# One square moved from VectorE to ScalarE at the end of the attention of batch 0

## The chip, the cores and the metric

One core of one Trainium2 chip. The metric is the device time of one execution in microseconds (us). Profiles were taken with each kernel. Positions inside a kernel are us from the start of the profiled span.

## The reference

```python
# q, k, v: (8 batches, 12 heads, 448 positions, 64)
scores = np.matmul(q, k.transpose(0, 1, 3, 2)) / np.sqrt(64)
attn   = np.maximum(scores, 0.0) ** 2 / 448        # ReLU, then a square; no softmax
x      = np.matmul(attn, v)                        # -> (3584 tokens, 768)
h      = x @ w_in                                  # 768 -> 2048
g      = np.maximum(h, 0) + alpha * np.minimum(h, 0)
out    = g @ w_out                                 # 2048 -> 768
```

## The kernel before

Heads are taken in quads (four heads of one batch; three quads make a batch), and a quad's scores in seven chunks `j`. A chunk runs through three engines: TensorE makes the scores, ScalarE or VectorE takes the ReLU into a bf16 tile `rl`, and the square goes into `at`, from which TensorE makes the product with V. Squares are done in pairs, two chunks in one VectorE instruction. Batch 0 has 21 chunks, so the last, chunk 6 of quad 2, is left without a partner, and is squared alone:

```python
def squares(keep=0, single=None):

    while len(todo) >= 2 + keep or todo and single is not None:
        m = min(len(todo), 2)
        some = [todo.pop(0) for _ in range(m)]
        t = some[0][2]
        a = at_pool.tile([128, 2, 2, S], BF16, tag="at", name="at")
        if m == 2:
            nc.vector.tensor_tensor(a, t, t, ALU.mult)                       # line 196
        else:
            cur.clear()
            if single is nc.scalar:
                nc.scalar.activation(a[:, 0], t[:, 0], ACTF.Square)          # line 200
            else:
                nc.vector.tensor_tensor(a[:, 0], t[:, 0], t[:, 0], ALU.mult) # line 202
        ...
def attnv(n, js=range(NJ), space=sc_ps, apart=False):
    ...
    for j in js:
        a = att.pop((n, j))
        for r in range(2):
            for s in range(2):
                nc.tensor.matmul(half[r][64 * s:64 * s + 64, :S],            # line 223
                                 vb[n][64 * r:64 * r + 64, s, j, :],
                                 a[64 * r:64 * r + 64, s],
                                 start=(j == 0), stop=(j == NJ - 1))
    ...  # then the rescale into xT, half on ScalarE (line 232), half on VectorE (line 234)
```

The end of batch 0's attention, with the first matmuls of the MLP put among it:

```python
# last quad, last chunks:
            if last and j > 4:
                ffn1(0, j - 5, range(0, 4))
            if last and j == 6:
                ffn1(0, 2, range(0, 4))
...
    squares(single=nc.vector)              # the line that changes
    attnv(2, range(0, 4), apart=True)
    attnv(2, range(4, NJ))
    ffn1(0, 3, range(0, 4))
...
    for ff in range(4):
        ffn1(0, ff, range(4, KM))          # these need the rescaled product
```

## Time and profile before

| | before |
|---|---|
| median, range of 3 runs | 390.79 us, 390.65 to 391.74 us |
| profiled span | 389.6 us |
| TensorE busy | 97% |
| VectorE / ScalarE busy | 65% / 55% |
| granted clock of TensorE | 1.0 |

What matters is not these shares but one place, 22 to 29 us, in the view of instructions in order of time; the prediction below shows it. A line there has the start, the duration, the engine, the source line, the operation, its output and inputs, the number of merged instructions, and, in brackets, how long the engine was idle before and what ended that.

One more number is the time from the start of the last two groups of MLP matmuls ahead of the product (eight matmuls of line 255; 23.23 us in the kernel before) to the first matmul of the MLP's second layer (line 271). From the view in order of time, 44 to 56 us, of the kernel before:

```profile
45.41 1.46 PE L271 MATMUL ops<-w_out_sb,gT 128*128 128x384 bf16 x8
```

The **stretch** is 45.41 - 23.23 = 22.18 us.

### The profile page before, as it was taken

What the parts mean: (1) busy time and instruction counts of PE and PEld (TensorE: products, weight loads), DVE (VectorE), ACT (ScalarE), POOL (GpSimd) and SP (SyncE); (2) the same over time, 40 slices, a digit from 0 to 9 for tenths busy, and PEclk for the clock granted to TensorE, in tenths of its full rate; (3) what the DMA queues carried; (4) which work ended last, traced back from release to release, by engine and by line L of the source; (5) the groups of instructions that cost most, each with busy time, mean ns of one, the idle gap of its engine ahead of it and who ended that gap; (6) DMA issues with size and microseconds to landing.
All of it is one profiled execution on the core that took longest, in us unless ns stands there. A gap on an engine that the chain in (4) does not pass through costs nothing.

```text
span 389.6 us, 7873 instructions
## 1 busy us (share of the span) xinstructions
PE 379.5 (97%) x3210; PEld 214.8 (55%) x3210; DVE 253.2 (65%) x336; ACT 215.5 (55%) x361; POOL 74.9 (19%) x89
## 2 busy tenths in 40 slices
PE   6799999999999999999999999999999999999996
PEld 4345556545655456645665456654566545655564
DVE  4986877687687757766675666777676376726411
ACT  5965767464566656664473645756565366624200
POOL 7654000052251114201221012301030000000000
PEclk9999999999999999999999999999999999999999
DMA  8999997894995519825494354937253220130033
GB/s 163 191 209 204 204 216 264 235 300 100 259 258 182 126 65 240 222 65 164 94 260 150 67 164 98 278 126 174 29 91 87 70 47 2 42 81 2 0 82 81
DMA packets 64755, 55.43 MB, mean 142 GB/s; under 512 B 35776, under 2 KB 60496, under 8 KB 64720
## 3 DMA queue, kind: packets, MB, share of 16 engines
q1 hardware_dynamic: 53504, 44.78, 44.7%
q0 software_dynamic: 10976, 9.96, 16.1%
q8 instruction: 25, 0.41, 0.4%
q10 hardware_dynamic: 240, 0.20, 0.2%
q14 instruction: 10, 0.08, 0.1%
HBM read 45.62 MB, written 11.01 MB: 145 GB/s over the span
## 4 chain that ended last, share of the span: by engine, by line
PE 93%; ACT 2%; DMA 2%; DVE 1%; POOL 1%; issue 0%; POOLq 0%; DVEq 0%
PE hps L255 37%; PE ops L271 37%; PE avh L223 7%; PE sc L156 6%; PE sch L156 3%; DMA qe<-in_q_dram 2%; PE ops L294 1%; PE av L223 1%; PE tps L131 1%; ACT rl L185 1%; DVE at L196 1%; ACT xT L232 0%; POOL ke L357 0%; POOL ke L355 0%; POOL qe L355 0%
## 5 line engine op out<-in xcount | busy, mean ns | idle before, releaser
L255 PE MATMUL hps<-xT,w_in_sb 128*128 128x448 bf16 x768 | 149.2, 353 | 0.6 <-ACT xT L232 0.4
L271 PE MATMUL ops<-w_out_sb,gT 128*128 128x384 bf16 x864 | 145.8, 326 | 0.0
L263 DVE SCALAR_TENSOR_TENSOR gT<-neg,beta_sb,hps 128x448 bf16<-128x448 f32 x128 | 85.7, 679 | 58.3 <-ACT neg L262 57.5
L271 PEld LDWEIGHTS <-gT 128*128 128x128 bf16 x864 | 83.4, 98 | 61.2 <-issue 7.9
L255 PEld LDWEIGHTS <-w_in_sb 128*128 128x128 bf16 x768 | 74.0, 98 | 72.5 <-issue 5.5
L262 ACT ACTIVATE neg<-hps 128x448 f32<-128x448 f32 x128 | 69.1, 546 | 63.7 <-PE hps L255 63.6
L185 ACT ACTIVATE rl<-sc 128x896 bf16<-128x896 f32 x87 | 77.1, 923 | 44.1 <-PE sc L156 44.0
L196 DVE TENSOR_TENSOR at<-rl 128x1792 bf16<-128x1792 bf16 x80 | 85.7, 1113 | 2.1 <-ACT rl L185 0.9
L106 DVE COPY osb<-ops 128x384 f32<-128x384 f32 x30 | 16.7, 557 | 45.6 <-PE ops L271 45.6
L163 ACT ACTIVATE rl<-sch 128x448 bf16<-128x448 f32 x81 | 41.6, 550 | 4.7 <-PE sch L156 4.6
L106 POOL CAST kb<-kraw 128x896 bf16<-128x896 f32 x16 | 18.8, 1178 | 114.5 <-DMA kT<-kb 55.9
L156 PE MATMUL sc<-qT,kT 64*64 64x448 bf16 x456 | 36.1, 355 | 3.1 <-ACT rl L185 1.4
L223 PE MATMUL avh<-at,vb 64*64 64x448 bf16 x588 | 34.4, 350 | 0.4 <-DVE at L196 0.4
L156 PEld LDWEIGHTS <-kT 64*64 64x64 bf16 x672 | 21.8, 106 | 19.6 <-issue 13.2
L104 ACT COPY osb<-ops 128x384 f32<-128x384 f32 x24 | 11.4, 476 | 36.0 <-PE ops L271 36.0
L223 PEld LDWEIGHTS <-vb 64*64 64x64 bf16 x672 | 25.7, 106 | 9.8 <-issue 5.2
L183 DVE TENSOR_SCALAR rl<-sc 128x896 bf16<-128x896 f32 x27 | 29.4, 1089 | 0.6 <-PE sc L156 0.6
L106 POOL CAST vb<-vraw 128x896 bf16<-128x896 f32 x16 | 15.9, 991 | 36.8 <-PE avh L223 36.7
L106 POOL CAST qb<-qraw 128x896 bf16<-128x896 f32 x16 | 16.6, 1040 | 32.3 <-DMA qT<-qb 28.0
L156 PE MATMUL sch<-qT,kT 64*64 64x448 bf16 x216 | 22.5, 355 | 0.0
L165 DVE TENSOR_SCALAR rl<-sch 128x448 bf16<-128x448 f32 x27 | 16.8, 622 | 2.8 <-PE sch L156 0.8
L238 DVE TENSOR_SCALAR xT<-avh 128x448 bf16<-128x448 f32 x19 | 11.9, 624 | 7.7 <-PE avh L223 7.7
(59 smaller groups left out, 98.4 us busy)
## 6 DMA issues: line engine op xcount, KB each, us to landing
out_dram<-osb SPq DMA_DIRECT2D x54, 192.0 KB, 2.8
qraw<-in_q_dram SPq DMA_DIRECT2D x19, 448.0 KB, 5.3
kraw<-in_k_dram SPq DMA_DIRECT2D x18, 448.0 KB, 4.4
vraw<-in_v_dram SPq DMA_DIRECT2D x18, 448.0 KB, 6.1
w_out_sb<-in_moe_w_out_dram POOLq DMA_DIRECT2D x2, 1536.0 KB, 20.0
w_in_sb<-in_moe_w_in_dram POOLq DMA_DIRECT2D x8, 192.0 KB, 8.7
w_in_sb<-in_moe_w_in_dram POOLq DMA_DIRECT2D x4, 384.0 KB, 9.8
vb<-in_v_dram POOLq DMA_DIRECT2D x6, 224.0 KB, 9.6
```

The lines of the kernel that those rows point to most:

```text
L106: eng.tensor_copy(o, i)
L156: nc.tensor.matmul(half[r][64 * c:64 * c + 64, :S], kT[n][64 * r:64 * r + 64, j, c, :], qT[n][64 * r:64 * r + 64, :, c, :], start=True, st ...
L163: nc.scalar.activation(rl[:, r], half[r][:, :S], ACTF.Relu)
L165: nc.vector.tensor_scalar(rl[:, r], half[r][:, :S], 0.0, None, ALU.max)
L183: nc.vector.tensor_scalar(rl, ps[:, :, :S], 0.0, None, ALU.max)
L185: nc.scalar.activation(rl, ps[:, :, :S], ACTF.Relu)
L196: nc.vector.tensor_tensor(a, t, t, ALU.mult)
L223: nc.tensor.matmul(half[r][64 * s:64 * s + 64, :S], vb[n][64 * r:64 * r + 64, s, j, :], a[64 * r:64 * r + 64, s], start=(j == 0), stop=(j ...
L255: nc.tensor.matmul(ps, w_in_sb[:, km // 2, km % 2, bass.ts(ff, 128)], xT[b][:, km // 2, km % 2, :], start=(km == 0), stop=(km == KM - 1))
L262: nc.scalar.activation(neg, ps, ACTF.Relu, scale=-1.0)
L263: nc.vector.scalar_tensor_tensor(gT[b // 2][:, ff, (b % 2) * S:(b % 2) * S + S], neg, beta_sb[:, ff:ff + 1], ps, ALU.mult, ALU.add)
L271: nc.tensor.matmul(ps, gT[sb][:, ff, bass.ts(c, 128)], w_out_sb[:, ff, bass.ts(hf, 384)], start=(ff == 0), stop=(ff == KF - 1))
```

## The change

The intent: at that place VectorE still has two pair squares to do before it comes to the single one, while ScalarE is done with its ReLUs and idle. ScalarE is to take it, so that the chunk is ready sooner.

```diff
-    squares(single=nc.vector)
+    squares(single=nc.scalar)
     attnv(2, range(0, 4), apart=True)
     attnv(2, range(4, NJ))
     ffn1(0, 3, range(0, 4))
```

## The prediction

> **What bounds the kernel now.** I read three things in order: the page's busy shares, the chain that ended last, and then the instructions in time order around the moved one.
>
> The busy shares:
>
> ```profile
> PE 379.5 (97%) x3210; PEld 214.8 (55%) x3210; DVE 253.2 (65%) x336; ACT 215.5 (55%) x361; POOL 74.9 (19%) x89
> ...
> PE 93%; ACT 2%; DMA 2%; DVE 1%; POOL 1%; issue 0%; POOLq 0%; DVEq 0%
> ```
>
> TensorE is busy 379.5 us of 389.6 us, and 93% of the chain that ended last is TensorE work. All idle time of TensorE together is 389.6 - 379.5 = 10.1 us, so a change that only moves vector work can win at most a part of these 10.1 us: the part that lies where it acts. Most of it lies in the first 22 us: the stretch 0 to 16 us has 11.41 us of TensorE work (4.6 us idle) and 16 to 22 us has 4.54 us (1.5 us idle). The stretch 24 to 28 us, where the moved instruction lies, has 4.00 us of TensorE work in 4.00 us.
>
> Now the instructions in order of time there. The two ReLU lines are from a window that shows the second of a merged pair apart; the rest is the opening 32 us:
>
> ```profile
> 23.35 0.92 ACT L185 ACTIVATE rl<-sc 128x896 bf16<-128x896 f32 x1
> 24.03 1.08 DVE L196 TENSOR_TENSOR at<-rl 128x1792 bf16<-128x1792 bf16 x1
> ...
> 23.23 1.69 PE L255 MATMUL hps<-xT,w_in_sb 128*128 128x448 bf16 x8
> 24.85 1.52 PE L223 MATMUL av<-at,vb 64*64 64x448 bf16 x28
> 25.04 0.62 DVE L202 TENSOR_TENSOR at<-rl 128x896 bf16<-128x896 bf16 x1
> 25.05 1.16 POOL L407 DMA_DIRECT2D w_out_sb<-in_moe_w_out_dram  x1 [0.28 <-DMA w_in_sb<-in_moe_w_in_dram]
> 26.30 2.44 PE L255 MATMUL hps<-xT,w_in_sb 128*128 128x448 bf16 x12
> 26.40 0.54 ACT L232 ACTIVATE xT<-av 128x448 bf16<-128x448 f32 x1 [2.13 <-PE av L223]
> 26.45 0.62 DVE L234 TENSOR_SCALAR xT<-av 128x448 bf16<-128x448 f32 x1 [0.79 <-PE av L223]
> ```
>
> What to see: the square of the last chunk (line 202, the only row of it here) starts on VectorE at 25.04, straight behind the two pair squares that VectorE still had to do, and ends at 25.66. ScalarE has made the chunk's ReLU by 23.35 + 0.92 = 24.27 and then stands idle for 2.13 us, until 26.40. So the operand is ready 0.77 us before VectorE comes to it, on an engine that has nothing else to do. That is plainly why one would move it.
>
> But TensorE has no gap there: 23.23 to 24.92, 24.85 to 26.37, 26.30 to 28.74 follow on each other without a wait. When does it need the chunk? The last quad's attention-times-V product is 28 matmuls, seven chunks of four, and the chunk in question is the seventh. The view by tile has the first of the 28 at 24.8 and the last at 26.0; evenly spread, 24.85 + 6 x (1.52 - 0.35)/6 = 26.02 us for the last group of four (0.35 us is one matmul's duration, the four of a group run side by side). Against 25.66 the square is ready **some 0.36 us before it is needed**. The list of what TensorE waited for between 22 and 60 us says the same; it is complete, and the square is not in it:
>
> ```profile
> PE hps L255 <- ACT xT L232: 0.4, 1, 0.4
> PE hps L255 <- DVE gT L263: 0.2, 1, 0.2
> ```
>
> The first of these is the wait at 22.05 for an earlier quad's rescaled output; the second is the wait at 28.96 for a PSUM buffer that the first activation of the MLP frees. Both have other producers than the moved square.
>
> **What the Trainium skill says.** "ScalarE: Activation LUTs", section "What ACT_TABLE_LOAD costs": an activation with immediate scale and bias takes 186 ns + 0.833 ns per element, so 932 ns for 896 elements; and every switch to another table set costs about 2.66 us. The trace agrees on the first: the six squares that ScalarE already does later in this kernel take 950 ns. On the second, the trace has a single table load, at 0.73 us, and those six squares run later without another, mixed with ReLUs and copies. So the new one needs no switch either:
>
> ```profile
> L200 ACT ACTIVATE at<-rl x6: 950/950/951, 112.9 to 339.4; 128x896 bf16<-128x896 bf16 x6
> L362 ACT ACT_TABLE_LOAD x1 | 1.3, 1283 | 0.7 <-PEq L555 0.7
> ```
>
> "VectorE: DVE Perf Modes", section "Side-by-side: where the cycles go for N=2048 bf16": two elements per cycle plus about 158 cycles for fill and decode, so (448 + 158)/0.96 = 631 ns for 896 bf16 elements; the trace has 618 to 626 ns for the two of them. So the operation becomes longer by about 0.33 us where it moves, and only its earlier start can make up for that.
>
> "SBUF — State Buffer", section "Who interferes with whom": VectorE with two SBUF inputs contends with GpSimd instructions that read SBUF. The moved square lay beside GpSimd's issue of the first half of the output weights (25.05, 1158 ns). The trace does not show a cost: the issue of the second half at 33.0, with no such square beside it, took 1158 ns too.
>
> "Perfetto Trace Analysis", section "Optimization Strategy": find the gaps of the engine that one optimizes for and what blocks it there. That is what the list above does; it finds no gap at this place.
>
> **The change part by part.** Built and compared instruction by instruction, the changed kernel has one row fewer on VectorE (line 202, 128x896), one more on ScalarE (line 200, between its last ReLU of the quad and the rescale of line 232), and the same TensorE, GpSimd and SyncE rows. The one altered wait is that of the first matmul of the last chunk: on ScalarE where it was on VectorE.
>
> - Removed from VectorE: 1 x 0.62 us, at 25.04 to 25.66. What VectorE does next is line 234, which waits for the end of the matmuls at 26.37 and starts at 26.45. So VectorE's idle time before it grows from 0.79 to about 1.3 us (26.45 less the 25.11 at which its last pair square ends), and line 234 starts as before. Worth 0.
> - Added to ScalarE: 1 x 0.95 us, from about 24.30 (the ReLU's end and a small semaphore delay) to 25.25. ScalarE's next is line 232 at 26.40, so its idle time there shrinks from 2.13 to about 1.1 us and line 232 starts as before. Cost 0.
> - The chunk is ready at about 25.25 instead of 25.66: 0.4 us earlier. The matmul that needs it starts at 26.02, because TensorE is then busy with the six chunks before. Slack 0.77 instead of 0.36 us. Gain 0.
> - Nothing behind it moves: the four matmuls end at 26.37 and the two rescales wait for that.
>
> The sum is 0 + 0 + 0 = **0.0 us**. The time stays at its 390.79 us; three runs of the same kernel lay between 390.65 and 391.74, so the range has to be that of the noise.
>
> **The rivals.**
>
> Rival 1, the chunk was on the path after all. TensorE's ends are modelled in the profile and the wait of the moved matmul could be hidden in the stated 1.52 us. For it: that the ends are modelled. Against: groups of 28 like it later in the chain take 1.47 us, this one 1.45 us, so it holds no hidden wait. If it were so, 0.1 to 0.4 us would be won: 390.4 to 390.7 us, 0.1%.
>
> Rival 2, ScalarE's square comes late or holds up the rescale of line 232, on which the next matmuls depend. For it: it is 0.33 us longer, and ScalarE is in order, so anything late in it delays line 232. Against: its operand is ready at 24.27, and it would have to end after 26.0 to hold up the matmul, after 26.4 to hold up the rescale; it would need to start 0.8 us late. If it did: up to +0.3 us.
>
> Rival 3, the timing of loads. The opening third is heavy with transfers (DMA engines busy nine tenths), and the first half of the output weights, issued at 25.05, takes 18.3 us, so lands at 43.4, 2.0 us before the first matmul that reads any of it at 45.4. If the missing VectorE instruction lets GpSimd write its descriptors sooner, that load could land a little earlier, but nothing waits for it now; the order of transfers does not change. Expected 0; through jitter of the opening loads (one DMA wait, 5.85 us from 4.32, is on the chain) several tenths of a us either way, in both kernels alike.
>
> Even if every one of these were added up, they stay under 1 us, or 0.25%; 2% is 7.8 us, over twelve times the whole instruction that was removed.
>
> **Range and chances.** Centre 390.8 us, the median before with a step of zero. The low end 390.1 allows rival 1 in full and a fast draw; the high end 391.8 allows a draw like the slowest of the three before, or rival 2. Within 2%: 0.98; faster and slower 0.01 each, for what I do not foresee.
>
> **What would show it right or wrong.** Right: in the profile after, line 200 on ScalarE at about 24.3 for 0.95 us; ScalarE's idle before line 232 down from 2.1 to about 1.1 us, VectorE's before line 234 up from 0.8 to about 1.3 us or a little more; the 28 matmuls still from 24.85 to 26.37 relative to the matmuls before them, with no TensorE wait for ScalarE's square; one table load; TensorE idle about 10 us in all. Wrong: a TensorE wait named after line 200 or longer than 0.1 us between 24 and 29 us; a second table load (about +1.3 to 2.7 us); matmuls of the last chunk that start clearly earlier than before, which would mean that the square had been on the path. A change of the total by over 1 us with this stretch unchanged would have to be noise or the opening loads.

## The result

| | before | after |
|---|---|---|
| median (6 runs each) | 390.92 us | 390.94 us |
| range | 390.5 to 391.74 us | 390.67 to 393.12 us |
| ratio, 95% interval | | 1.0008, 0.9986 to 1.0029 |

Ratios are the mean time of one kernel's runs over that of the other's of the same rounds, so not quite the ratio of the medians quoted. The time lies in the predicted range.

The profiled run of after happened to be the 393.12 us one, with a span of 391.3 us against 389.6. Its page, then instructions of it in order of time:

```profile
PE 381.7 (98%) x3210; PEld 215.7 (55%) x3210; DVE 251.7 (64%) x335; ACT 216.3 (55%) x362; POOL 74.9 (19%) x89
...
PEclk9699999999999999999999999999999999999999
```

```profile
24.91 1.69 PE L255 MATMUL hps<-xT,w_in_sb 128*128 128x448 bf16 x8
24.92 1.16 POOL L407 DMA_DIRECT2D w_out_sb<-in_moe_w_out_dram  x1 [0.26 <-DMA w_in_sb<-in_moe_w_in_dram]
25.98 0.95 ACT L200 ACTIVATE at<-rl 128x896 bf16<-128x896 bf16 x1
26.53 1.52 PE L223 MATMUL av<-at,vb 64*64 64x448 bf16 x28
28.09 0.54 ACT L232 ACTIVATE xT<-av 128x448 bf16<-128x448 f32 x1 [1.15 <-PE av L223]
28.13 0.62 DVE L234 TENSOR_SCALAR xT<-av 128x448 bf16<-128x448 f32 x1 [1.63 <-PE av L223]
...
47.09 1.46 PE L271 MATMUL ops<-w_out_sb,gT 128*128 128x384 bf16 x8
```

Read the last two views against those of before. The square is on ScalarE now (line 200, 0.95 us) and ends 0.40 us after the product's first matmul starts (25.98 + 0.95 - 26.53), where on VectorE it ended 0.81 us after (25.66 - 24.85). So the chunk **is** ready 0.41 us sooner. Yet the 28 matmuls take their 1.52 us as before, and the stretch is 47.09 - 24.91 = 22.18 us, to the hundredth what it was. What TensorE waits for from 22 to 60 us is the same two lines, 0.4 and 0.2 us, that the prediction shows for the kernel before.

All of the 1.7 us by which this span is longer lies ahead of the square: the MLP matmuls of the stretch start at 24.91 here and at 23.23 before (1.68 us). The row of granted clock goes with it: the second slice (about 10 to 20 us) reads 6, not 9. In slices of one microsecond the clock of after is 0.50 from 11 to 17 us, while that of before is 1.00 there. (This run also waits 1.5 us for a load at about 9 us; but behind it TensorE is only 0.22 us later than in before, at 10.43 against 10.21, so 1.46 us of the 1.68 come after it.) None of this can come from an instruction that starts at 26 us; the first experiment and a run of the kernel before itself (393.06 us, at the same mean clock of 0.989) confirm it.

### The profile page after: what moved, and what is told of

Same layout as the page of the kernel before. It is cut to its first block, busy times and chain, and to the rows that moved or that the text cites. A ratio compares the mean times of both kernels' runs of the same rounds, so it can differ in the third digit from the quotient of the medians.

```text
span 391.3 us, 7873 instructions
## 1 busy us (share of the span) xinstructions
PE 381.7 (98%) x3210; PEld 215.7 (55%) x3210; DVE 251.7 (64%) x335; ACT 216.3 (55%) x362; POOL 74.9 (19%) x89
## 4 chain that ended last, share of the span: by engine, by line
PE 95%; DMA 2%; ACT 1%; POOL 1%; issue 0%; DVE 0%; POOLq 0%
PE hps L255 37%; PE ops L271 37%; PE avh L223 8%; PE sc L156 6%; PE sch L156 3%; DMA qe<-in_q_dram 2%; PE ops L294 1%; PE tps L131 1%; PE av L223 1%; ACT rl L185 1%; ACT rl L163 0%; POOL ke L357 0%; POOL ke L355 0%; POOL qe L355 0%; DVE gT L263 0%
## 5 line engine op out<-in xcount | busy, mean ns | idle before, releaser
L196 DVE TENSOR_TENSOR at<-rl 128x1792 bf16<-128x1792 bf16 x80 | 84.8, 1103 | 2.1 <-ACT rl L185 0.9
L106 POOL CAST kb<-kraw 128x896 bf16<-128x896 f32 x16 | 19.7, 1230 | 117.0 <-DMA kT<-kb 53.9
L223 PE MATMUL avh<-at,vb 64*64 64x448 bf16 x588 | 35.5, 360 | 0.0
L106 POOL CAST vb<-vraw 128x896 bf16<-128x896 f32 x16 | 16.7, 1044 | 37.3 <-PE avh L223 37.1
L106 POOL CAST qb<-qraw 128x896 bf16<-128x896 f32 x16 | 15.0, 934 | 31.4 <-DMA qT<-qb 31.4
```

The costliest lines, as they stand in the source:

```text
L106: eng.tensor_copy(o, i)
L223: nc.tensor.matmul(half[r][64 * s:64 * s + 64, :S], vb[n][64 * r:64 * r + 64, s, j, :], a[64 * r:64 * r + 64, s], start=(j == 0), stop=(j ...
```

## The experiments

Ten kernels were run, 5 rounds each beside the kernel before on the same chip (4 to 6 runs of each). One execution of each was profiled, so a stretch is a single reading; those that should be alike differ by 0.01 us. Three views were read from each: the waits of TensorE, the instructions in order of time, and the stretch defined above. The theory, **S**: the square has slack on both engines, so its move buys nothing. The rivals: **C**, it is on the path and the profile hides it; **B** and **A**, as told with each run.

### The changed kernel once more

No edit.

> The changed kernel once more, for a profile whose opening ran at full granted clock (the first one had 0.84 there). Theory S (slack): the moved square was ready before TensorE needed it on either engine, so the time is that of before, ratio 1.000 within 0.002; counted from the first matmul of the last quad's attention-times-V product, the square ends at +0.40 us on ScalarE (it ended at +0.81 on VectorE) and the last four matmuls still begin at +1.17. Rival C (critical after all): faster by 0.1 to 0.4 us. Rival N (the 1.7 us longer span of the first profile belongs to the change and not to the clock): the span is again near 391.3 us at a clock of 1.0.

Median 390.75 us (390.61 to 390.81) against 390.93 (390.5 to 391.22); ratio 0.9995, interval 0.9983 to 1.0008; span 388.9 us, clock 0.999. In order of time:

```profile
22.55 1.69 PE L255 MATMUL hps<-xT,w_in_sb 128*128 128x448 bf16 x8
23.62 0.95 ACT L200 ACTIVATE at<-rl 128x896 bf16<-128x896 bf16 x1
24.17 1.52 PE L223 MATMUL av<-at,vb 64*64 64x448 bf16 x28
25.72 0.55 ACT L232 ACTIVATE xT<-av 128x448 bf16<-128x448 f32 x1 [1.15 <-PE av L223]
25.77 0.62 DVE L234 TENSOR_SCALAR xT<-av 128x448 bf16<-128x448 f32 x1 [1.33 <-PE av L223]
...
44.73 1.46 PE L271 MATMUL ops<-w_out_sb,gT 128*128 128x384 bf16 x8
```

The stretch is 44.73 - 22.55 = 22.18 us, again the same. Rival N falls: at a clock of 1.0 the longer span is gone. The idle time ahead of line 232 on ScalarE is 1.15 us (2.13 before) and that ahead of line 234 on VectorE 1.33 us (0.79 before): the work went into the one and came out of the other.

### No square at all

```diff
-                nc.vector.tensor_tensor(a[:, 0], t[:, 0], t[:, 0], ALU.mult)
+                a = t          # simplified: this chunk only; wrong result on purpose
```

> The square of the chunk is left out altogether (the product takes the ReLU unsquared; a wrong result on purpose). This is the most that any move of it could win. Theory S: 0.0 us, ratio 1.000 within 0.002, no change in TensorE's waits from 22 to 60 us. Rival C: faster by 0.1 to 0.4 us or more.

The result is wrong (relative error 0.44). Median 390.84 us (390.8 to 391.04); ratio 0.9999, interval 0.9986 to 1.0012; the stretch 45.04 - 22.87 = 22.17 us:

```profile
22.87 1.69 PE L255 MATMUL hps<-xT,w_in_sb 128*128 128x448 bf16 x8
24.49 1.33 PE L223 MATMUL av<-at,vb 64*64 64x448 bf16 x24
25.65 0.36 PE L223 MATMUL av<-rl,vb 64*64 64x448 bf16 x4
...
45.04 1.46 PE L271 MATMUL ops<-w_out_sb,gT 128*128 128x384 bf16 x8
```

TensorE's waits from 22 to 60 us are again the same two. So this is the ceiling: whoever does this square, and however fast, can win nothing. Rival C, which asked for 0.1 to 0.4 us, gets 0.01 in the stretch; the interval of the time alone would still allow it. The last four matmuls have a line of their own here, as their input has another name: with no square to wait for they start at 25.65 - 24.49 = +1.16 us, where the prediction had worked out +1.17 from even spacing.

### Three squares on ScalarE, and three on VectorE

How much slack is there? The square is repeated into a scratch tile ahead of the true one, on either engine.

```diff
+                for i in range(2):   # and the same with nc.vector.tensor_tensor
+                    nc.scalar.activation(junk[:, i], t[:, 0], ACTF.Square)
                 nc.scalar.activation(a[:, 0], t[:, 0], ACTF.Square)
```

> ScalarE squares the chunk three times, the true one last (the result stays right). Two more at about 0.86 us apart make it ready at about +2.1 us after the first matmul of the product, needed at +1.17. Theory S: a TensorE wait of about 0.95 us named after line 200 appears, that is 1.72 added less 0.77 of slack; the time grows by about 0.95 us (ratio 1.0024). Rival C (no slack): the wait and the time grow by 1.7 us (1.0044). Rival A (a later gap takes it up again): a wait, but no longer time.

> VectorE squares the chunk three times, the true one last, as the kernel before does once. Two more at about 0.53 us apart make it ready at about +1.87 us after the first matmul of the product, needed at +1.17. Theory S: slack on VectorE is only 0.36 us, so a TensorE wait of about 0.7 us appears and the time grows by 0.7 us (ratio 1.0018). Rival C (no slack): 1.06 us (1.0027).

On ScalarE: median 391.66 us against 390.93, ratio 1.0019, interval 1.0007 to 1.0032. The stretch is 46.11 - 22.94 = 23.17 us, so +0.99. In order of time:

```profile
24.56 1.33 PE L223 MATMUL av<-at,vb 64*64 64x448 bf16 x24
25.70 0.93 ACT L200 ACTIVATE at<-rl 128x896 bf16<-128x896 bf16 x1
26.69 0.38 PE L223 MATMUL av<-at,vb 64*64 64x448 bf16 x4 [0.80 <-ACT at L200]
```

On VectorE: median 391.85 us against 390.9, ratio 1.0023, interval 1.0011 to 1.0035. The stretch is 45.67 - 22.71 = 22.96 us, so +0.78:

```profile
24.32 1.33 PE L223 MATMUL av<-at,vb 64*64 64x448 bf16 x24
25.58 0.62 DVE L202 TENSOR_TENSOR at<-rl 128x896 bf16<-128x896 bf16 x1
26.25 0.38 PE L223 MATMUL av<-at,vb 64*64 64x448 bf16 x4 [0.60 <-DVE at L202]
```

Now the last group of four is torn from the 24 before it, and the wait has the name of the square. (The wait is less than the delay because it counts from the end of the matmuls before, which overlap with the next when nothing holds them.) The delays tell the slack. On ScalarE the square was ready at +2.07 us after the first matmul and not at +0.40, so 1.67 us later; the delay was 0.99, so 0.68 us had been slack. On VectorE +1.88 and not +0.81, so 1.07 later, the delay 0.78, slack 0.29 us. The prediction had 0.77 and 0.36; the difference, 0.09 and 0.07, is about the hand-over that it left out (0.05 to 0.06 us from the square's end to the matmul in the lines above). The waits expected, 0.95 and 0.7 us, came out as 0.80 and 0.60. Rival C, delays of 1.7 and 1.06 us, falls for both by the stretch; by the time alone it falls on ScalarE only, since its 1.0027 lies inside VectorE's interval. The delay comes back nowhere (from line 271 to the end of the span are 344.2 us here and before), which speaks against rival A.

### The chunk taken first

If the chunk came first in the product, its square would be on the path. Does the move then pay?

```diff
     squares(single=nc.vector)                     # first_dve; nc.scalar in first_act
-    attnv(2, range(0, 4), apart=True)
-    attnv(2, range(4, NJ))
+    attnv(2, range(NJ), apart=True, order=[6, 0, 1, 2, 3, 4, 5])
```

(with start and stop of the accumulation set on the first and last of that order).

> The square stays on VectorE, but the product takes this chunk first, not last (the sum of seven chunks in another order; the result stays right). Theory S: now it is needed at +0 and ready at +0.81 plus a small delay, so TensorE waits about 0.85 us for line 202, and the time grows by as much (ratio 1.002). Rival C: the order does not matter, no new wait.

> The change together with the order that takes this chunk first. Theory S: ready at +0.40 plus a small delay, so TensorE waits about 0.44 us for line 200; against the same order with VectorE the move wins about 0.41 us, which is what it was to win but could not where the chunk comes last. In the time that is 0.1%, near the noise, so the waits in the profile decide. Rival B (ScalarE is no earlier, because the ReLUs ahead of it shift): the waits of the two are alike.

The chain of waits, for VectorE and then for ScalarE (what TensorE waited for, total us, times, longest):

```profile
PE av L223 <- DVE at L202: 0.8, 1, 0.8
```

```profile
PE av L223 <- ACT at L200: 0.4, 1, 0.4
```

On VectorE the stretch grows by 0.85 us (45.61 - 22.58 = 23.03) and the time has a ratio of 1.0021, interval 1.0009 to 1.0033, median 391.70 us. On ScalarE the stretch grows by 0.44 us (45.60 - 22.98 = 22.62), with a ratio of 1.0012, interval 0.9999 to 1.0025, median 391.47 us. Both are what theory S gave to the hundredth. So the move does buy its 0.41 us where the chunk is waited for; in the kernel as it is, the order of the chunks had already bought more than that. In the total time the two intervals overlap, and the difference of 0.23 us between the medians alone would not show it; the traces do. Rival B falls.

### Eight squares, five squares

These were to test that lateness beyond the slack counts one to one, with an effect far above the noise.

```diff
-                for i in range(2):
+                for i in range(7):   # act8, dve8; range(4) in act5
```

> ScalarE squares the chunk eight times, the true one last. Added 7 x 0.86 = 6.0 us, less 0.77 of slack: theory S expects a TensorE wait of about 5.25 us and as much in the time (ratio 1.013). Rival C: 6.0 us (1.0154). Rival A: clearly under 5 us in the time though the wait is over 5 us.

> VectorE squares the chunk eight times, the true one last. Added 7 x 0.53 = 3.7 us, less 0.36 of slack: theory S expects a TensorE wait of about 3.35 us and a ratio of 1.0086. Rival C: 3.7 us, 1.0095.

ScalarE: 397.94 us against 390.93, ratio 1.0179 (1.0165 to 1.0193). VectorE: 395.6 us against 390.9, ratio 1.0124 (1.0103 to 1.0145). Both are **above both theories**: about 7.0 us where 5.25 was expected and rival C had 6.0, and by the mean 4.85 us where S had 3.35 and C 3.7. The six runs with eight on VectorE are not alike, and their times go with their mean granted clocks: 394.49 and 394.7 us at 0.999 and 1.0, 395.43 and 395.78 at 0.995 and 0.996, 396.92 and 397.39 at 0.991 and 0.989. The first two are 3.6 and 3.8 us above the kernel before, close to S. The waits are nearly as S said (5.25 and 3.35):

```profile
PE av L223 <- ACT at L200: 5.0, 1, 5.0
```

So the excess comes after the wait. The instructions of the run with eight on VectorE that was profiled (395.43 us):

```profile
28.44 0.59 PE L223 MATMUL av<-at,vb 64*64 64x448 bf16 x4 [3.27 <-DVE at L202]
28.96 3.61 PE L255 MATMUL hps<-xT,w_in_sb 128*128 128x448 bf16 x12
```

Four matmuls take 0.59 us and not 0.38, and the next twelve 3.61 and not 2.44 us: 0.21 + 1.17 = 1.38 us more. The wait put the last group at 28.44 - 23.83 = +4.61 us, 3.44 late; 3.44 + 1.38 = 4.82 us, and the stretch (49.17 - 22.22 = 26.95) has grown by 4.77. The sum is closed: TensorE itself had become slow. In slices of one microsecond its granted clock reads 0.50 from 28 to 31 us (with eight on ScalarE, from 31 to 34). "TensorE: Matmul & The Clock Gate" of the Trainium skill, section "Part 1: The HAM clock gate (the "warmup" mystery)", tells of this: a monitor halves the array's clock after an idle window of about 3.4 us and restores it after a busy one. Two more runs were made to see whether it is that:

> ScalarE squares the chunk five times, the true one last. From the waits already measured (0.80 us for three squares, 5.00 us for eight: 0.84 us per square) the wait of TensorE is 2.48 us. Eight squares cost 7.0 us where the wait was 5.0, because the granted clock then read 0.50 for about 3.5 us behind the wait. Theory K (the clock falls only after a long idle, and is what the excess is): two ways are open. If an idle of 2.5 us is short enough, the time grows by 2.5 us (ratio 1.0064) at a clock of 1.00; if not, the clock reads 0.50 behind it and the time grows by 4 us or more (1.010). Theory L (the excess is a fixed share of the wait, 7.0/5.0, whatever the clock does): 3.5 us (1.009) with a clock of 1.00.

Five squares: median 394.89 us against 391.0, ratio 1.0098 (1.0085 to 1.0112); the stretch grew by 3.99 us (49.03 - 22.86 = 26.17). TensorE's wait was 2.48 us, as expected, and the clock fell all the same. Busy time in slices of one microsecond (columns: slice, length; busy us of TensorE matmuls, weight loads, VectorE, ScalarE, GpSimd; granted clock; transfers' share and GB/s):

```profile
27.00:28.00 1.00, 0.00 (x0) 0.00 (x0) 0.00 (x0) 1.00 (x2) 0.70 (x1) 0.98 1.14 213
28.00:29.00 1.00, 0.71 (x5) 0.26 (x5) 0.05 (x1) 0.33 (x2) 0.00 (x0) 0.50 1.14 213
29.00:30.00 1.00, 1.00 (x4) 0.40 (x3) 0.57 (x1) 0.45 (x1) 0.71 (x1) 0.50 1.11 203
30.00:31.00 1.00, 1.00 (x4) 0.36 (x3) 0.00 (x0) 0.00 (x0) 0.29 (x1) 0.50 1.21 203
31.00:32.00 1.00, 1.00 (x6) 0.48 (x5) 0.16 (x1) 0.73 (x2) 0.43 (x1) 0.81 1.22 198
```

A mean of 0.98 between 1.00 and 0.50 puts the fall at about 27.96 us, 0.81 the return at about 31.38 us: 3.4 us at half clock. How long TensorE had then been idle differs: some 2.2 us here, 2.8 with eight on VectorE (27.94 - 25.16), 5.0 with eight on ScalarE (30.84 - 25.85). So the length of the idle alone does not set the moment of the fall. One of the four runs here (394.48 us) had a mean clock of 1.0 and was still 3.5 us above the kernel before, where the lateness (28.29 - 24.48 = +3.81 and not +1.17) is 2.64 us; its trace was not kept, and this stays open. Theory L, a fixed share without a lower clock, expected 3.5 us at a clock of 1.00. Only that one run would fit it; it falls by the clock and the time of the profiled run (395.05 us, +4.05) and by the next experiment.

### Eight squares, with TensorE kept busy

```diff
+    attnv(2, range(0, 6), apart=True)
+    hps[3] = mm_ps.tile(...)      # the tile that ffn1(0, 3) then overwrites
+    for _ in range(44):
+        nc.tensor.matmul(hps[3][:, :256], warm_w, warm_x, start=True, stop=True)
+    attnv(2, range(6, NJ))
```

> As the run with eight squares, but TensorE fills its wait with 44 matmuls of the kernel's dummy operands (128x256[...]) into a PSUM tile that the next true matmul overwrites, so it is idle for 0.3 us and not for 5.0. The square comes as late as before. Theory K: the clock stays at 1.00, the excess goes, and the time grows by the lateness alone, 5.0 us (ratio 1.013). Theory L, or any cause of the excess other than an idle TensorE: the time still grows by 7.0 us (1.018).

Median 395.92 us against 391.0, so +4.9 us. The mean ratio, 1.0142 (1.0119 to 1.0165), has one run of 398.29 us in it; the other four lie between 395.77 and 396.21 us. That one run had a clock of 0.999, and why it was slow stays open. In order of time:

```profile
25.43 4.98 PE L411 MATMUL hps<-warm_x,warm_w 128*128 128x256 bf16 x44
29.51 0.93 ACT L200 ACTIVATE at<-rl 128x896 bf16<-128x896 bf16 x1
30.50 0.38 PE L223 MATMUL av<-at,vb 64*64 64x448 bf16 x4
30.81 2.44 PE L255 MATMUL hps<-xT,w_in_sb 128*128 128x448 bf16 x12
```

The four matmuls are back to 0.38 us and the twelve to 2.44, and the clock reads 1.00 in every slice from 26 to 35 us. The stretch grew by 5.19 us (49.92 - 22.55 = 27.37), against 6.50 us (51.58 - 22.90 = 28.68) without the dummies: 1.31 us of excess are gone, and what is left is the lateness (the last group at +6.33 us and not +1.17, so 5.16 late). So theory K holds for the profiled runs: the excess is the clock, and it comes from TensorE standing idle, not from the lateness as such.

## Why the prediction was right

The prediction was 390.8 us with a step of zero; measured was 390.94 us and a ratio of 1.0008 with 1 inside its interval.

- **TensorE has no gap there.** Shown: its waits from 22 to 60 us are the same two lines in before, after and with no square at all.
- **The operation gets longer, but ready sooner.** 0.95 for 0.62 us, ready at +0.40 for +0.81 us: as worked out (25.25 - 24.85 = 0.40).
- **The chunk is needed at +1.17 us, so there is slack of 0.36 us before and 0.77 after.** Shown by the runs with three squares, as 0.29 and 0.68 us, and by the one without a square, where the chunk's matmuls start at +1.16; the hand-over between the engines had been left out.
- **VectorE's idle grows to about 1.3 us, ScalarE's shrinks to about 1.1.** 1.33 and 1.15 us in the clean profile. In the first profile of after VectorE's was 1.63, because there the pair squares ended at 26.49 us, 0.04 us before the product's first matmul, where in the clean profile they ended 0.26 us after it.
- **The sum is 0.** The stretch is 22.18, 22.18 and 22.18 us in before, after and after once more, and 22.17 with no square.
- **Rival 1 (on the path after all)** fell with the run without a square; **rival 2 (ScalarE late)** with the slack of 0.68 us; of **rival 3 (loads)**, GpSimd's issue of the output weights took 1.16 us in both kernels. The changed kernel once more shows it without a VectorE square beside it: the issue runs from 24.85 to 26.01 us, and VectorE is idle from 24.43 to 25.77. (In the first profile of after the pair squares lay beside it, so that one cannot tell.) Its jitter of the opening is real and is larger than the prediction said: not several tenths but 2.2 us in the two runs with a clock of 0.989 (393.12 us of after, 393.06 us of before). Whether the loads brought the clock down is not shown. One of the six runs lay far above the range; the median saved it, which is partly luck.
- **Its signs.** One table load in after, as said, and 391.3 - 381.7 = 9.6 us of idle TensorE. One sign of being wrong was ill-set: a wait "longer than 0.1 us between 24 and 29 us" stands in the kernel before too, 0.21 us at 28.96 for line 263, so it could not have told anything.

What was off was one expectation after it: that lateness beyond the slack counts one to one at any size. It does for 0.4 to 1 us. Behind an idle of 2.5 us and more the clock fell in all three kernels profiled, and that added 1.33 to 1.35 us; with eight squares on VectorE, two of the six runs show that it need not fall each time.

## What to carry to other kernels

Before moving an instruction to an idle engine, find the instruction that consumes it and when that one could start at the earliest; a producer that already finishes sooner than that buys nothing by being faster, unless the engine that it leaves comes sooner to something that is waited for. Here VectorE's next instruction waited for the same product. What comes last in an accumulation has the slack of all that comes before it, so the order of the chunks does the same work as a faster producer, and does it for free. And when a delay is tested by making it large, look at the granted clock behind it: a longer idle of TensorE can cost more than its length, and not in every run.

## What the Trainium skill lacked or had wrong

- "TensorE: Matmul & The Clock Gate", section "Why this matters for your kernels", advises against idle gaps of over about 3 us. Here a wait of 2.48 us was enough: the clock fell at about 27.96 us, some 2.2 us after the end of the matmuls before it (24.48 + 1.33 = 25.81). With eight squares it fell 2.8 and 5.0 us after that end, and in two of six runs with eight on VectorE the mean clock shows no fall. Waits of 0.60 and 0.80 us left it at 1.00. In the first profile of after it read 0.50 from 11 us on, though no wait of TensorE before that was over 1.5 us. The length of the half clock, 3.4 us, agrees with the page's window. The page does not say how little work within a window counts as idle; no run here measures it.
- "ScalarE: Activation LUTs", section "Rules for kernel authors", says to use VectorE and not ScalarE for a multiply. By duration that holds here (0.62 against 0.95 us), but the slower engine had the result ready 0.41 us sooner, because it was free; the rule says nothing of that. The estimate for one activation by the formula in its section "What ACT_TABLE_LOAD costs", 932 ns, measured 950 ns.
- No page says how a slack behind TensorE is measured by repeating the producer; the runs with three squares found 0.29 and 0.68 us so, to within 0.1 us of what was read from the trace.
